# Zero pieces between the experts' weights, scatters issued as results come, and thirteen zero pieces ahead of the experts

## The chip, the cores and the metric

One core of a Trainium2 chip runs the whole kernel. The metric is the device time of one execution in microseconds (us); for the kernel before the median of three runs is shown. TensorE is called PE, VectorE DVE, ScalarE ACT, GpSimd POOL and SyncE SP, as the profile does; SP does nothing here but issue transfers, and POOL issues those with indices.

## The reference

Attention over 8 batches, 8 heads, 576 positions of 64 values, with a window of 128 and a bias by distance, and behind it a layer of experts on the 4608 tokens of 512 values: each token goes to the expert of its highest logit, an expert keeps the 80 tokens of highest gate weight, and every row of the output that no expert keeps is zero.

```python
attn_out = _attn_ref(q, k, v)
x = attn_out.transpose(0, 2, 1, 3).reshape(B * S, H * D)
logits = x @ w_gate
expert_idx = np.argmax(logits, axis=1)
out = np.zeros((N, D))
for e in range(E):
    tok_idx = np.where(expert_idx == e)[0]
    if len(tok_idx) > capacity:
        ...                        # the 80 of highest gate weight
    h = np.maximum(x[tok_idx] @ w1[e], 0.0)
    out[tok_idx] = gate_w[tok_idx, None] * (h @ w2[e])
```

## The kernel before, in words

The kernel has three stages. The attention runs as 72 units, nine to a batch; while the units of one batch run, the inputs of the next are loaded, the tokens of the one before are stored to a scratch tensor `x_dram`, and the choice of the 80 tokens of each expert is merged batch by batch. Behind the last unit comes the passage, in which the choice for the last batch is finished; a chain of small steps on DVE, ACT and PE, with idle matmuls between them. Then the eight experts run one after the other on PE: first layer (128 matmuls, line 1332), second layer (line 1358), three partial sums copied by ACT (line 1360) and the fourth added by DVE (line 1367), which makes the result `ys` of 80 rows of 512 values.

Around the experts the transfers are these. The tokens of each expert are gathered from `x_dram` by POOL (`gather`, line 1267). The weights of an expert are 4 MB (`expert_pieces`, line 656): four pieces of 512 KB for w1 and four for w2, issued by SP in this order; there is room for four experts, and the weights of expert e + 4 are issued behind the second layer of expert e (`load_expert`, lines 1361 to 1363). A result goes to the output by an indexed transfer of POOL (`scatter`, line 1312). The output must be zero elsewhere, so 36 pieces of 128 rows (256 KB each, source the tile `zero`) are written over it before any scatter may write; the scatters write to the same tensor in no known place, so each is ordered behind all writes to the output issued before it.

The list `fill` (lines 1074 to 1079) holds what SP issues when there is room: 32 half pieces of the weights of experts 0 and 1, the zero piece for the first rows of `x_dram`, and the 36 zero pieces of the output, 69 in all. `transfers(c)` (line 1132) gives up to three transfers to unit c of the attention, each with a lead, an instruction of the unit that it may not pass (`pace`, line 238); a place without a load or store takes the next of `fill`, as long as more than `LATE` are left (line 1167). The lists of `transfers` have 36 such places, so that 33 pieces are left at the end of the attention and lines 1219, 1220, 1227 and 1228 issue none. The 33 are issued all at once behind the weights of expert 7 (lines 1364 and 1365). Seven scatters are issued behind the first layer of the last expert (lines 1339 to 1341), the eighth at the end (line 1371).

Attention and passage are not issued as written. They are recorded, and a planner (`order`, line 255) puts them in order with a model of each engine's clock: at each step it takes, on the engine that can start first, the recorded operation with the lowest place in the code among those that are ready by then:

```python
t0 = max(clock[e], min(r for r, _ in rs))
...
o = min((o.key, o.at, i) for i, (r, o) in enumerate(rs) if r <= t0 + self.slack)
```

A transfer is ready when its lead, if it has one, and the operations that wrote its source are done in the model. The tile `zero` is cleared by `selection_constants` (line 637), called for unit 3. The experts are issued as written.

Of the kernel before, what the change touches and what calls it, by code (L numbers as in the profile page):

```python
# [24 lines left out]
FREE = ()  # L25

FAST = (7,)
LATE = 33


class Plan:
# [362 lines left out]
def tile_attention_then_moe(  # L394
# [15 lines left out]
    B, NP, _, S = q.shape  # L410
    H = 2 * NP
    E, DM, DF = w1.shape
# [103 lines left out]
    def load_v(b, i):  # L516
        w = H * VW
        rows = LOW if 2 * i + 1 == NKB else ALL
        return nc.sync.dma_start(
            out=vts[b % 2][rows, i].rearrange("p h c -> p (h c)"), in_=v[b][rows, w * i:w * i + w])  # L520

    def load_vt(b, g):
        if g == 0:
            vtt[b] = io.tile([P, NP, S], F32, tag="vtt", name=f"l_vt{b}", bufs=1)
        return nc.sync.dma_start(out=vtt[b][:, g], in_=vt[b, g])

    def load_k(b, g, a=0, c=S):
        return nc.sync.dma_start(out=kps[(b * NP + g) % NQ][:, a:c], in_=k[b, g, :, a:c])

    def load_q(b, g, a=0, c=S):  # L530
        if a == 0:
            qs[b, g] = io.tile([P, S], F32, tag="q", name=f"q{b}_{g}", bufs=NQ)
        return nc.sync.dma_start(out=qs[b, g][:, a:c], in_=q[b, g, :, a:c])
# [112 lines left out]
    def put_kept(b, i, k=0):  # L646
        kp = spare(i, k).bitcast(BF16)
        twice(kp[:, 0:R], at, 0, identb[0:R, 0:R])
        yield
        (nc.scalar.copy if b == LAST else nc.vector.tensor_copy)(ttt[b % 2][:, S:S + R], kp[0:2 * KS, 0:R])  # L650
# [5 lines left out]
    def expert_pieces(e, n=1):  # L656
        pool = wpools[e % 4 // 2]
        a = pool.tile([P, NC, DF], F32, tag="w1", name=f"w1_{e}")
        c = pool.tile([P, PW, DM], F32, tag="w2", name=f"w2_{e}")
        w_sb[e] = (a, c)  # L660
        s1 = w1[e].rearrange("(c p) f -> p c f", p=P)
        s2 = w2[e].rearrange("(c p) f -> p c f", p=P)

        def one(dst, src):
            return lambda: nc.sync.dma_start(out=dst, in_=src)

        w = DF // n
        m = 2 // n
        return ([one(a[:, j, w * h:w * h + w], s1[:, j, w * h:w * h + w]) for j in range(NC) for h in range(n)]
                + [one(c[:, m * j:m * j + m], s2[:, m * j:m * j + m]) for j in range(PW // m)])  # L670

    def load_expert(e):
        for piece in expert_pieces(e):
            piece()
# [182 lines left out]
    def store_x(b, u):  # L857
        return [
            nc.sync.dma_start(
                out=x_dram[P + S * b + 64 * t:P + S * b + 64 * t + 64],  # L860
                in_=xsb[b % 2][64 * j:64 * j + 64, u].rearrange("p h c -> p (h c)"))
            for j, t in enumerate(SLOT[u])]
# [211 lines left out]
    fill = []  # L1074
# [5 lines left out]
    nexp = 2  # L1080
# [6 lines left out]
    def whole(g):  # L1087
        for _ in g:
            pass
# [42 lines left out]
    def transfers(c):  # L1132
        b, r = divmod(c, CB)
        n = b + 1
        vt_ = [lambda g=g: load_vt(n if r < 8 else n + 1, g) for g in range(NP)]
        v_ = [lambda i=i: load_v(n, i) for i in range(NPR)]
        k_ = [lambda g=g: load_k(n, g) for g in range(NP)]
        q_ = [lambda g=g: load_q(n, g) for g in range(NP)]
        x_ = [lambda u=u: store_x(b - 1, u) for u in range(NU)] if b else [None] * NU
        at_ = {  # L1140
            0: [vt_[1], vt_[2]],
            1: [vt_[3], v_[0], None],
            2: [v_[1], k_[0], x_[0]],
            3: [q_[0], k_[1], x_[1]],
            4: [q_[1], v_[2], x_[2]],
            5: [v_[3], v_[4], x_[3]],
            6: [k_[2], q_[2], x_[4]],
            7: [k_[3], q_[3]],
            8: [vt_[0], None],
        }[r]  # L1150
        if b == 0 and r < 8:
            at_ = {
                2: vt_[0:1], 3: vt_[1:4], 4: [k_[0], q_[0], v_[0]], 5: [v_[1], k_[1], q_[1]],
                6: v_[2:5], 7: [k_[2], q_[2], k_[3]],
            }.get(r, [])
        elif b == 0:
            at_ = [q_[3], vt_[0], None]
        if b == LAST:
            at_ = [q for q in at_ if q in x_] + [None] * 3
            if r == 7:  # L1160
                at_ = [lambda: store_x(b, 0)] + at_
        elif b == LAST - 1 and r == 8:
            at_ = [None] * 3
        out_ = []
        for q in at_[0:3]:
            if q is None:
                q = fill.pop(0) if len(fill) > LATE and c > 4 else None
            if q:
                out_.append(q)
        return out_  # L1170
# [13 lines left out]
    for c in range(1, NCY):  # L1184
# [5 lines left out]
        if c == 3:  # L1190
            make_first_bias(2)
            make_first_bias(3)
            selection_constants()
        moves = transfers(c)
        if moves:
            nc.pace(moves.pop(0)(), marks["t", c, 1])
# [21 lines left out]
    whole(put_kept(LAST, 0))  # L1218
    for _ in range(min(4, len(fill) - LATE)):
        fill.pop(0)()  # L1220
# [4 lines left out]
    for u in range(1, NU):  # L1225
        store_x(LAST, u)
    while len(fill) > LATE:
        fill.pop(0)()
# [24 lines left out]
    def ps(tag, bufs, name):  # L1253
        return psum.tile([P, 512], F32, tag=tag, bufs=bufs, name=name)
# [44 lines left out]
    for e in range(2):  # L1299
        first = gather(e)  # L1300
    while nexp < 4:
        for piece in expert_pieces(nexp):
            tc.add_manual_dep(
                piece().ins, first.ins.name,
                mybir.DependencyInfo(mybir.DependencyClass.Sync, mybir.DependencyReason.DATA),
                reason="the first tokens before more weights")
        nexp += 1
# [4 lines left out]
    def scatter(e, ys):  # L1312
        nc.gpsimd.indirect_dma_start(  # L1313
            out=out, out_offset=bass.IndirectOffsetOnAxis(ap=sid[:, e:e + 1], axis=0),
            in_=ys, in_offset=None,
            bounds_check=NTOK - 1, oob_is_err=False,
        )

    ready = []
    for e in range(E):  # L1320
        a, c = w_sb.pop(e)
        xgT = xgTs.pop(e)
        nxt = turn(e + 1, 1) if e + 1 < E else None
        hT = work.tile([P, PW, R], F32, tag="hT", name=f"hT{e}", bufs=2)
        for f2 in range(PW // 4):
            hp = ps("s", NS, f"h{e}_{f2}")
            for fi in range(4):
                fc = 4 * f2 + fi
                for cc in range(NC):
                    for hh in range(2):  # L1330
                        f0 = P * fc + 64 * hh
                        nc.tensor.matmul(  # L1332
                            hp[64 * hh:64 * hh + 64, R * fi:R * fi + R],
                            lhsT=a[:, cc, f0:f0 + 64], rhs=xgT[:, cc],
                            start=(cc == 0), stop=(cc == NC - 1),
                        )
            nc.scalar.activation(  # L1337
                hT[:, 4 * f2:4 * f2 + 4].rearrange("p c r -> p (c r)"), hp[:, 0:4 * R], AF.Relu)
        if e == E - 1:
            for done in ready:  # L1340
                scatter(*done)
        groups = [(m0, min(R, m0 + 32)) for m0 in range(0, R, 32)]
        spread = len(groups) == 3
        own = PW * 3 // 4 if spread else PW
        yp = ps("pt", NPT, f"y{e}")
        ex = [ps(t, n, f"yx{e}_{t}") for t, n in (("d", ND), ("o", NO), ("s", NS))] if spread else []
        ys = work.tile([R, DM], F32, tag="ys", name=f"ys{e}", bufs=E)
        if nxt:
            nxt()
        for r in range(own):  # L1350
            mms = [(yp[m0:m1, 0:DM], PW - own + r, m0, m1, r == 0, r == own - 1) for m0, m1 in groups]
            if spread:
                j = r // 2
                m0, m1 = groups[j]
                mms.insert(3 * (1 - r % 2), (
                    ex[j][96:96 + m1 - m0, 0:DM], r % 2, m0, m1, r % 2 == 0, r % 2 == 1))
            for o, f_, l0, l1, st, sp in mms:
                nc.tensor.matmul(o, lhsT=hT[:, f_, l0:l1], rhs=c[:, f_], start=st, stop=sp)  # L1358
            if spread and r % 2:
                nc.scalar.copy(ys[m0:m1], ex[j][96:96 + m1 - m0, 0:DM])  # L1360
        if nexp < E:
            load_expert(nexp)
            nexp += 1
        while fill and nexp == E:
            fill.pop(0)()
        if spread:
            nc.vector.tensor_tensor(ys, ys, yp[0:R, 0:DM], ALU.add)  # L1367
        else:
            nc.vector.tensor_copy(ys, yp[0:R, 0:DM])
        ready.append((e, ys))  # L1370
# [45 lines left out]
```

## Time and profile before

| | us |
|---|---|
| median of 3 runs | 338.61 |
| lowest, highest | 338.28, 341.62 |
| profiled execution | 337.49 |
| its span, first to last instruction | 335.7 |

The profile is of one execution. Its page shares the span in 40 slices of 8.4 us and gives for each the busy share of the engines in tenths and the rate of the transfers. A busy share is an average over stages of different kinds, so a stretch is read by itself. An indexed transfer shows in POOL's timeline while it is issued; its data lands later, and the view of the transfers gives the median time from the start of the issue to the landing.

### The profile page before, as it was taken

Reading aid. Unit: us, or ns where it says so; the run is one execution under the profiler, and the core shown is the slowest. Engines: PE = TensorE matmul, PEld = TensorE weight load, DVE = VectorE, ACT = ScalarE, POOL = GpSimd, SP = SyncE. Lnnn points to the kernel's source line nnn. Section 1 sums busy time; section 2 is a strip of 40 time slices with the busy share of each in tenths; the row PEclk is TensorE's granted clock in tenths of the full one; section 3 lists DMA queues with packets and bytes.
Section 4 is the critical chain, followed back from the end, with each engine's and each line's share of the span. In section 5 each row is a group of like instructions: output and inputs, shape, how many; then the busy total and the mean of one; then the engine's idle time right before and its main releaser. Section 6 shows DMA issues by size and latency. Waiting matters only on the chain. (4 is left out here: it accounts for less than half of the span.)

```text
span 335.7 us, 15531 instructions
## 1 busy us (share of the span) xinstructions
PE 291.6 (87%) x6333; PEld 212.9 (63%) x6333; DVE 171.4 (51%) x970; ACT 160.8 (48%) x489; POOL 134.9 (40%) x358
## 2 busy tenths in 40 slices
PE   8899999999999999999999999999999999940000
PEld 6577767788778778787787788646665557610000
DVE  5566777888888789788787974101111101000000
ACT  8485766767665766667667731132222322220000
POOL 8644654855846746657558503600000000001322
PEclk9999999999999999999999999999999999995555
DMA  7969999899998998989989993799999999995121
GB/s 216 350 206 313 353 297 312 260 305 305 270 316 283 301 301 275 289 272 324 296 283 345 293 331 87 240 299 398 395 394 396 400 398 391 364 369 195 39 59 39
DMA packets 46278, 97.01 MB, mean 289 GB/s; under 512 B 5504, under 2 KB 6144, under 8 KB 46208
## 3 DMA queue, kind: packets, MB, share of 16 engines
q1 hardware_dynamic: 45184, 93.22, 81.6%
q0 software_dynamic: 1024, 2.81, 3.2%
q8 instruction: 50, 0.82, 1.0%
q14 instruction: 20, 0.16, 0.2%
HBM read 74.19 MB, written 21.81 MB: 286 GB/s over the span
## 5 line engine op out<-in xcount | busy, mean ns | idle before, releaser
L360 POOL TENSOR_SCALAR e<-e,mn 128x192 f32<-128x192 f32 (+2 forms) x216 | 87.1, 417 | 66.7 <-DVE mn L360 55.4
L360 ACT ACTIVATE ptb<-pt 128x384 f32<-128x384 f32 x144 | 64.7, 475 | 51.0 <-PE pt L360 50.1
L360 PE MATMUL av<-v,ptb 128*64 128x73 f32 (+1 forms) x2048 | 81.5, 235 | 0.9 <-issue 0.8
L360 DVE CUSTOM_DVE_ANT_0 e<-s,bneg 128x192 f32<-128x192 f32 x192 | 61.4, 354 | 35.1 <-PE s L360 26.6
L360 PEld LDWEIGHTS av<-v,ptb 128*64 128x64 f32 (+1 forms) x2048 | 64.4, 135 | 12.1 <-issue 1.3
L360 PE MATMUL s<-kp,q 64*64 64x192 f32 (+2 forms) x1152 | 60.4, 313 | 1.5 <-DMA q<-in_q_dram 1.5
L1313 POOL DMA_INDIRECT out_dram<-ys,sid x8 | 7.4, 920 | 107.7 <-DMA out_dram<-zero 90.4
L360 ACT COPY xs<-av 128x146 f32<-128x146 f32 (+1 forms) x176 | 42.9, 284 | 4.4 <-PE av L360 3.3
L1367 DVE TENSOR_TENSOR ys<-ys,y 80x512 f32<-80x512 f32 x8 | 5.5, 683 | 76.5 <-ACT ys L1360 76.5
L1358 PE MATMUL y<-w,hT 128*32 128x512 f32 (+1 forms) x288 | 43.4, 594 | 0.5 <-issue 0.5
L360 PEld LDWEIGHTS s<-kp,q 64*64 64x64 f32 x1152 | 39.1, 132 | 3.4 <-issue 1.6
L360 PE MATMUL pt<-ident,e 64*128 64x64 f32 (+1 forms) x832 | 41.0, 229 | 0.1
L1332 PEld LDWEIGHTS h<-xgTs,w 128*64 128x64 f32 x1024 | 35.9, 137 | 6.5 <-issue 6.0
L360 PEld LDWEIGHTS pt<-ident,e 64*128 64x128 f32 (+1 forms) x832 | 31.5, 135 | 11.8 <-POOL kk L360 3.1
L1332 PE MATMUL h<-xgTs,w 128*64 128x80 f32 x1024 | 37.2, 233 | 0.4 <-ACT xgTs L1296 0.4
L360 ACT ACTIVATE e<-e,mn 128x192 f32<-128x192 f32 (+1 forms) x72 | 31.2, 433 | 6.1 <-DVE mn L360 3.7
L1358 PEld LDWEIGHTS y<-w,hT 128*32 128x32 f32 (+1 forms) x288 | 10.8, 105 | 25.8 <-issue 24.8
L360 DVE DVE_READ_ACCUMULATOR2_ANT mn<- 128x1 f32 x288 | 23.9, 83 | 0.1
L360 DVE TENSOR_SCALAR_CACHE_REDUCE ncm<-s 128x272 bf16<-128x272 f32 (+7 forms) x68 | 22.7, 382 | 1.1 <-PE s L360 1.0
L1337 ACT ACTIVATE hT<-h 128x320 f32<-128x320 f32 x16 | 7.0, 437 | 29.1 <-PE h L1332 29.1
L360 DVE CUSTOM_DVE_ANT_0 e<-s,bnx 128x192 f32<-128x192 f32 (+2 forms) x64 | 17.5, 304 | 3.9 <-ACT ptb L360 3.0
L1358 PE MATMUL yx_d<-w,hT 128*32 128x512 f32 x32 | 15.2, 598 | 0.0
(144 smaller groups left out, 310.8 us busy)
## 6 DMA issues: line engine op xcount, KB each, us to landing
w<-in_moe_w_dram SPq DMA_DIRECT2D x48, 512.0 KB, 10.8
x_dram<-xs SPq DMA_DIRECT2D x72, 146.0 KB, 4.2
v<-in_v_dram SPq DMA_DIRECT2D x32, 292.0 KB, 5.0
l_vt<-in_vt_dram SPq DMA_DIRECT2D x32, 288.0 KB, 4.1
out_dram<-zero SPq DMA_DIRECT2D x36, 256.0 KB, 4.2
kp<-in_k_dram SPq DMA_DIRECT2D x31, 288.0 KB, 4.6
q<-in_q_dram SPq DMA_DIRECT2D x31, 288.0 KB, 4.9
w<-in_moe_w_dram SPq DMA_DIRECT2D x32, 256.0 KB, 4.5
```

Source lines behind the costliest of these rows:

```text
L360: c.ins = c.f(*c.args, **c.kw)
L1313: nc.gpsimd.indirect_dma_start(out=out, out_offset=bass.IndirectOffsetOnAxis(ap=sid[:, e:e + 1], axis=0), in_=ys, in_offset=None, bounds_c ...
L1332: nc.tensor.matmul(hp[64 * hh:64 * hh + 64, R * fi:R * fi + R], lhsT=a[:, cc, f0:f0 + 64], rhs=xgT[:, cc], start=(cc == 0), stop=(cc == NC ...
L1337: nc.scalar.activation(hT[:, 4 * f2:4 * f2 + 4].rearrange("p c r -> p (c r)"), hp[:, 0:4 * R], AF.Relu)
L1358: nc.tensor.matmul(o, lhsT=hT[:, f_, l0:l1], rhs=c[:, f_], start=st, stop=sp)
L1367: nc.vector.tensor_tensor(ys, ys, yp[0:R, 0:DM], ALU.add)
```

## The change

Of the 33 zero pieces that are left at the end of the attention, the lines behind the last attention unit now issue 13: four ahead of `keep_clock` and nine behind the stores of the last tokens. Twenty are left. Eight are issued behind the weights of expert 3; like those weights, they wait for the second gather. Six follow the weights of expert 4, six those of expert 5, so that the list is empty behind expert 1's second layer. A result is scattered behind the first layer of a later expert, as soon as the list is empty: results 0 and 1 in expert 2, result e - 1 in expert e. The attention takes the same 36 pieces of `fill` as before. Which zero piece goes where is not told by the rows that it clears.

```diff
-LATE = 33
+LATE, GAPS = 20, 13
...
-                q = fill.pop(0) if len(fill) > LATE and c > 4 else None
+                q = fill.pop(0) if len(fill) > LATE + GAPS and c > 4 else None
...
-        for piece in expert_pieces(nexp):
+        for piece in expert_pieces(nexp) + [fill.pop(0) for _ in range(8 * (nexp == 3))]:
             tc.add_manual_dep(
                 piece().ins, first.ins.name,
...
-        if e == E - 1:
-            for done in ready:
-                scatter(*done)
+        while ready and not fill:
+            scatter(*ready.pop(0))
...
         if nexp < E:
             load_expert(nexp)
             nexp += 1
-        while fill and nexp == E:
+        for _ in range(min(6, len(fill))):
             fill.pop(0)()
```

The lines behind the last attention unit are not changed; they follow from the smaller `LATE`:

```python
    for _ in range(min(4, len(fill) - LATE)):
        fill.pop(0)()
    keep_clock(nc.last, 150)
    ...
    for u in range(1, NU):
        store_x(LAST, u)
    while len(fill) > LATE:
        fill.pop(0)()
```

## Rows read from the trace of the kernel before

**Rows 1.** The page: span, PE in 40 slices, and the DMA's rate in them.
```profile
span 335.7 us, 15531 instructions
...
PE   8899999999999999999999999999999999940000
...
GB/s 216 350 206 313 353 297 312 260 305 305 270 316 283 301 301 275 289 272 324 296 283 345 293 331 87 240 299 398 395 394 396 400 398 391 364 369 195 39 59 39
```

**Rows 2.** Timeline of the tail: start, duration (us), engine, line [idle before it <- releaser].
```profile
298.05 0.68 DVE L1367 TENSOR_TENSOR ys<-ys,y 80x512 f32<-80x512 f32 x1 [9.18 <-ACT ys L1360]
...
307.92 0.95 POOL L1313 DMA_INDIRECT out_dram<-ys,sid  x1 [90.43 <-DMA out_dram<-zero]
...
331.61 0.91 POOL L1313 DMA_INDIRECT out_dram<-ys,sid  x1 [2.47 <-issue]
```

**Rows 3.** The scatter's line: durations in ns (least, median, most), and landing in us.
```profile
L1313 POOLq EVENT_SEMAPHORE  x12: 17/2776/2813, 304.5 to 328.1; - x12
...
DMA to landing us min/median/max: 2.6/2.6/2.6
```

**Rows 4.** Timeline of SP: the weights' first row, and the zero pieces.
```profile
212.29 27.28 SPq L665 DMA_DIRECT2D w<-in_moe_w_dram  x22
...
275.05 29.07 SPq L1079 DMA_DIRECT2D out_dram<-zero  x33
```

**Rows 5.** Windows: stretch, each engine's busy time (instructions), PE's clock, DMA share, GB/s.
```profile
core 0: us, PE busy (x) PEld busy (x) DVE busy (x) ACT busy (x) POOL busy (x), PEclk, DMA share, GB/s
...
220.00:225.00 5.00, 4.56 (x44) 1.57 (x46) 0.00 (x0) 1.16 (x2) 0.00 (x0) 1.00 1.03 283
225.00:270.00 45.00, 45.00 (x817) 28.05 (x812) 6.73 (x10) 13.18 (x26) 0.00 (x0) 1.00 1.04 396
```

**Rows 6.** Timeline of PE: the first layers of experts 6 and 7.
```profile
277.18 4.65 PE L1332 MATMUL h<-xgTs,w 128*64 128x80 f32 x128
...
287.47 4.65 PE L1332 MATMUL h<-xgTs,w 128*64 128x80 f32 x128
```

**Rows 7.** SP's issue of four weight pieces, and times to landing, in the same order.
```profile
252.80 0.37 SPq L665 DMA_DIRECT2D w<-in_moe_w_dram  x1
...
257.93 0.33 SPq L665 DMA_DIRECT2D w<-in_moe_w_dram  x1
...
w<-in_moe_w_dram SPq DMA_DIRECT2D x1, 512.0 KB, 10.5
...
268.41 0.33 SPq L665 DMA_DIRECT2D w<-in_moe_w_dram  x1
...
w<-in_moe_w_dram SPq DMA_DIRECT2D x1, 512.0 KB, 11.3
...
273.77 0.37 SPq L665 DMA_DIRECT2D w<-in_moe_w_dram  x1
...
w<-in_moe_w_dram SPq DMA_DIRECT2D x1, 512.0 KB, 11.5
```

**Rows 8.** Landing of the gathers issued at 210.2, 212.7 and 216.5 us.
```profile
xg<-x_dram,gid POOLq DMA_INDIRECT x1, 3.1
...
xg<-x_dram,gid POOLq DMA_INDIRECT x1, 8.6
...
xg<-x_dram,gid POOLq DMA_INDIRECT x1, 9.1
```

**Rows 9.** Early: the zero tile's memset, SP's next issue, and two windows as above.
```profile
14.56 0.58 POOL L360 MEMSET zero<- 128x584 f32 x1
...
17.27 4.36 SPq L360 DMA_DIRECT2D l_vt<-in_vt_dram  x4
...
15.00:20.00 5.00, 5.00 (x113) 3.68 (x113) 3.89 (x23) 2.59 (x10) 2.62 (x7) 1.00 0.70 207
20.00:25.00 5.00, 5.00 (x135) 3.83 (x128) 2.40 (x16) 4.57 (x16) 2.48 (x6) 1.00 0.68 227
```

**Rows 10.** Window behind PE's last work, columns as above.
```profile
301.20:302.00 0.80, 0.00 (x0) 0.00 (x0) 0.00 (x0) 0.00 (x0) 0.00 (x0) 0.54 1.02 384
```

## Prediction

> **What bounds the kernel now.** I read the page first: its span and its forty slices [rows 1]. PE is at 9 tenths until about 297 us and stands still for the last 38 us, while the DMA moves 364 to 400 GB/s from 227 us until about 302 us and in the last three slices 39 to 59 GB/s. The end is therefore no matter of compute. The timeline of the tail says what it is [rows 2]: the last expert's result is added on DVE at 298.05 and is ready at 298.7, but the first of the eight scatters starts at 307.92, released by the DMA of the zero pieces, and the eighth at 331.61. Seven steps take 23.7 us, 3.38 us each. The group of the scatter's line [rows 3] shows why they don't overlap: a scatter lands 2.6 us after its start, and its sequencer sits 2.78 us on a semaphore between two of them, so each scatter waits until the one before has landed, and about 0.75 us go by from the landing to the next start (3.38 less 2.6). From the last start to the end of the span are 4.1 us.
>
> SP's timeline [rows 4] gives the order of the transfers: weights from 212.29, 33 zero pieces from 275.05. The windows [rows 5] give the rate of that stream: 396 GB/s from 225 to 270 with PE busy in all of it. So a zero piece (262144 bytes) is 0.66 us of DMA, 33 of them 21.8 us, and both streams, PE's and the DMA's, are full at once. The tail of 37 us (298.7 to 335.7) is 9.2 us of waiting for zeros, 23.7 us of chained scatters, and 4.1 us of end.
>
> **The zeros that leave the tail.** Thirteen pieces move ahead of the experts, twenty go between weights: eight behind expert 3, six behind expert 4, six behind expert 5. All twenty are ahead of expert 6 in SP's one queue. Expert 5's last piece was issued at 252.80 and landed 10.5 us later, at 263.3 [rows 7]; with twenty zeros ahead of or just behind it the last zero lands at 263.3 + 20 x 0.66 = 276.5 instead of about 307. The first scatter can start at 276.5 + 0.75 = 277.3; results 0 to 5 are there by then or a microsecond later.
>
> **What the twenty cost the experts.** Expert 6's first layer needs its four w1 pieces, the last issued at 257.93 and landed 10.5 us later, 268.4; now 268.4 + 13.2 = 281.6. Its first matmul was at 277.18 [rows 6], so PE waits 4.4 us where it had 8.8 us in hand. Expert 7's w1 was complete at 268.41 + 11.3 = 279.7 [rows 7], now at 292.9 and with one scatter's 164 KB (0.4 us) 293.3; it would start at 287.47 + 4.4 = 291.9, so 1.4 us more. Expert 5 is on the edge: its w1 comes one expert (4.19 MB at 396 GB/s, 10.6 us) ahead of expert 6's in the old order, at 257.8, now 14 zeros or 9.3 us later at 267.1, and it starts 10.29 us ahead of expert 6, at 266.9. Expert 4, another 10.6 and 10.29 us earlier, has eight zeros, 5.3 us, against 9.4 in hand: nothing. In all PE ends 5.8 us later, and the last result is ready at 298.7 + 5.8 = 304.5.
>
> In that wait PE does a pair of matmuls per landed piece and no more. In the tail of before the granted clock had fallen from the upper to the lower level by 301.2 to 302 (mean 0.54), about 4 us behind PE's last work [rows 10]. If it falls in the wait of expert 6 too, its first layer (4.65 us) takes up to twice as long: the result at 309.2. As will be seen, that still lies ahead of the scatter that waits for it.
>
> **What the earlier scatters cost.** They are issued from POOL, which has nothing else to do here, so a blocked scatter blocks nobody. But now they run while SP keeps eight weight pieces of 512 KB in flight, and they stay chained, since all write the same tensor. The trace has no scatter under load. Its nearest rows are the gathers, the same kind of transfer on the same queue [rows 8]: 3.1 us alone, 8.6 us for the first one issued after the weights had begun, 9.1 us for the last. From below the bound is the 2.6 us of a lone scatter, from above the 9.1 us. I take the gather's 8.6 less the half microsecond by which a lone scatter is quicker: 8.1, a step of 8.85 us.
>
> The weights end at 273.77 + 11.5 = 285.3 [rows 7], now 285.3 + 13.2 + 0.8 (two scatters' data) = 299.3. Then: scatter 0 at 277.3, 1 at 286.1, 2 at 295.0. The third has only 4 us of load left, between 2.6 and 8.1: I take 5.0, so scatter 3 at 300.8. From there on 3.38 each: 304.1, 307.5, 310.9, and scatter 7 at 314.3. Its result was ready at 304.5 (309.2 with a fallen clock), so the chain decides and the wait of PE is hidden under it. End: 314.3 + 4.1 = 318.4, against 335.7: 17.3 us less.
>
> A rule bears on this. The Trainium skill, "DMA: Bandwidth & Descriptors", section "Queues, rings and completion order", says that each DMA engine takes turns between the queues that have work, one packet at a time. By it a scatter wouldn't stand behind what SP has outstanding, its step would stay near that of a lone one, and the end would be the one of the first rival below. The trace speaks against it so far: the gather's 8.6 us beside 3.1.
>
> **The thirteen.** They are named "in the passage", in the code behind the last attention unit. But the planner orders each queue by what is ready, and these pieces have no lead and read only the zero tile, so they are ready as soon as its memset is done, at 15.1 us [rows 9]. A piece with a lower place in the code wins when both are ready; the zeros fill each idle moment of SP. I expect them from about 15 us on, among the loads of the second batch, where SP idles between loads and the DMA engines are busy only 0.70 and 0.68 of the time [rows 9]. From 15 to 25 us about 3.1 us of DMA are free, five zeros; the other eight, 5.3 us, are spread over later gaps or push loads back. Price: from nothing to 5.3 us if all of the rest reached PE; loads are issued two or three units ahead, so I take 0.5 us. Wherever they go, they leave the tail; their 8.6 us are in the 13.2 against 21.8 above.
>
> **Sum.** 335.7 - 17.3 + 0.5 = 318.9 us of span, 16.8 less. The profiled execution took 337.49 (1.8 beyond its span), so 320.7 for it; the median of the runs shown is 338.61, 1.1 more. On the median: 338.61 - 16.8 = 321.8, predicted 322.
>
> **Rivals.** (1) Scatters stay short under load, by the rule of turns. With 2.6 us the chain would be at its eighth at 277.3 + 7 x 3.38 = 301.0, before the last result; the end is then PE's: 304.5 + 0.4 + 4.1 = 309.0, with 0.5 for the loads 26.2 less, 312.4. With a step of 5 us, midway: scatters at 277.3, 282.3, 287.3, 292.3, 297.3 and from 301.5 on by 3.38, eighth at 308.3, end 312.4, total 315.8. For it: a scatter moves only 164 KB, 0.4 us at the stream's rate; against it: [rows 8].
> (2) The thirteen do stand in the passage, or the loads pushed back reach PE. In the passage the DMA has a hole (one slice of 87 GB/s) [rows 1], but four pieces go ahead of the last token stores, 2.6 us, and the gathers behind nine more would land later than 3.1 us, by up to the 5.5 us between a lone and a loaded one [rows 8]. The experts start 1.5 to 6 us later: 323 to 328.
> (3) Slower than before: zeros written and scattered between weights break the stream. From 220 to 225, with gathers among the weights, it ran at 283 GB/s instead of 396 [rows 5]. The stream from 212.3 is 32 MB (48 weight pieces, 20 zeros, six gathers, some scatters), 23 MB of it up to the last zero. At 283 GB/s that zero lands at 293.5, the weights end at 325, three scatters take 8.85 us each, the fourth 5.75, and the eighth starts at about 337: end 341, a total of 344. At 300 GB/s the eighth starts at 331.6, as before: that is the point from which it decides. Against it: the dip lasted 5 us.
>
> **Chances.** The forecast, chain under load, 319.5 to 326: 0.60. Short scatters, 311 to 319.5: 0.24. Passage or late loads, 323 to 332: 0.11, half of it within the first's span. Broken stream: 0.05. The range holds the first two and what of the third lies near: 312 to 327. A change of about 1% is what a measurement of this kernel can tell from none; faster by over 1% (under 335.2) is all but the last case and a sliver: 0.94, the same 0.03, slower 0.03.
>
> **What would show it.** Scatter 0 starts near 277 and the next ones about 9 us apart while weights flow, then 3.4; PE waits for weights before experts 6 and 7 and not before; the last scatter starts over 5 us behind the last add; thirteen zero pieces stand in SP's timeline between 15 and 60 us. I am wrong if scatters under load land in under 5 us, if the last add is what releases the last scatter, or if PE waits for loads in the attention for more than 3 us.

## The result, and the profile after

The changed kernel takes 324.39 us (median of four runs, 323.02 to 325.47) beside 338.62 us for the kernel before: a ratio of 0.956 (95% interval 0.949 to 0.962). The profiled execution took 324.34 us with a span of 322.6. Predicted were 322, with 318.9 for the span. A ratio is taken over fewer executions than the median beside it (unusually slow ones are left out), so it is not exactly the quotient of two medians.

The page of the changed kernel, in the lines of [rows 1] and with PE's clock:

```profile
span 322.6 us, 15529 instructions
...
PE   9999999999899999999999999998999999959930
...
PEclk9999999999989999999999999999999999988985
...
GB/s 223 362 304 345 340 317 297 330 321 316 318 255 279 342 316 285 267 268 299 322 284 289 329 272 317 285 59 277 320 400 393 364 396 401 402 403 402 243 45 41
```

PE now works until about 309 us, 13 us before the end (38 us in the kernel before), and the stretch at 39 to 59 GB/s behind the zeros has become two slices at 41 to 45. PE's clock dips in slice 12 and in slices 36 and 37, where it was even before. The hole of the passage is still there, at 59 GB/s.

The timeline of the changed kernel, with the lines that answer to [rows 2]: the first gather, the scatters on POOL, and the last add on DVE.

```profile
212.82 1.19 POOL L1270 DMA_INDIRECT xg<-x_dram,gid  x1 [3.80 <-DVE sid L1261]
...
283.41 0.95 POOL L1313 DMA_INDIRECT out_dram<-ys,sid  x1 [60.42 <-DMA w<-in_moe_w_dram]
290.02 0.93 POOL L1313 DMA_INDIRECT out_dram<-ys,sid  x1 [5.66 <-issue]
297.29 0.91 POOL L1313 DMA_INDIRECT out_dram<-ys,sid  x1 [6.33 <-issue]
304.47 0.91 POOL L1313 DMA_INDIRECT out_dram<-ys,sid  x1 [6.27 <-issue]
308.30 0.91 POOL L1313 DMA_INDIRECT out_dram<-ys,sid  x1 [2.92 <-issue]
...
309.79 0.68 DVE L1366 TENSOR_TENSOR ys<-ys,y 80x512 f32<-80x512 f32 x1 [9.18 <-ACT ys L1359]
...
318.46 0.91 POOL L1313 DMA_INDIRECT out_dram<-ys,sid  x1 [2.48 <-issue]
```

The chain of scatters starts at 283.4 instead of 307.9, its first three steps are 6.6, 7.3 and 7.2 us long instead of 3.4, and its last scatter still starts eight microseconds behind the last result (310.5). So the chain sets the end, as before. The first row tells of something else: the first gather starts at 212.8, 5.4 us later than in the kernel before, though nothing of the attention's own work has changed. The same row of the kernel before:

```profile
207.41 1.19 POOL L1270 DMA_INDIRECT xg<-x_dram,gid  x1 [3.79 <-DVE sid L1261]
```

### The profile page after: what moved, and what is told of

Read it like the earlier page. It is cut to its first block, busy times and chain, and to the rows that moved or that the text cites. A ratio compares the mean times of both kernels' runs of the same rounds, so it can differ in the third digit from the quotient of the medians.

```text
span 322.6 us, 15529 instructions
## 1 busy us (share of the span) xinstructions
PE 297.9 (92%) x6333; PEld 217.0 (67%) x6333; DVE 171.2 (53%) x970; ACT 160.8 (50%) x489; POOL 134.4 (42%) x358
## 5 line engine op out<-in xcount | busy, mean ns | idle before, releaser
L360 PE MATMUL s<-kp,q 64*64 64x192 f32 (+2 forms) x1152 | 61.9, 316 | 1.0 <-DMA q<-in_q_dram 0.5
L1332 PEld LDWEIGHTS h<-xgTs,w 128*64 128x64 f32 x1024 | 37.8, 141 | 10.8 <-issue 6.6
L1332 PE MATMUL h<-xgTs,w 128*64 128x80 f32 x1024 | 39.7, 239 | 4.0 <-DMA w<-in_moe_w_dram 3.0
L360 PE MATMUL pt<-ident,e 64*128 64x64 f32 (+1 forms) x832 | 42.0, 230 | 0.6 <-issue 0.4
L360 PEld LDWEIGHTS s<-kp,q 64*64 64x64 f32 x1152 | 39.8, 133 | 3.8 <-issue 1.4
```

What stands on the lines that cost most here:

```text
L360: c.ins = c.f(*c.args, **c.kw)
L1332: nc.tensor.matmul(hp[64 * hh:64 * hh + 64, R * fi:R * fi + R], lhsT=a[:, cc, f0:f0 + 64], rhs=xgT[:, cc], start=(cc == 0), stop=(cc == NC ...
```

## Experiments

Times are medians of four or six runs; each ratio is to the kernel before on the same chip. Single executions of the kernels below lie up to 1.4% to either side of their median. A profile is of one execution, so a difference of two or three microseconds in one profile is read only together with the others.

**The thirteen left out.**

```diff
-    for _ in range(min(4, len(fill) - LATE)):
-        fill.pop(0)()
...
-    while len(fill) > LATE:
-        fill.pop(0)()
+    del fill[:GAPS]
```

> The thirteen zero pieces that the changed kernel issues among the loads of the attention are left out altogether (1664 rows of the output are not cleared by the kernel); all else is as changed. Theory A: these transfers are what makes the attention 5.4 us longer in the changed kernel (gathers from 212.8 instead of 207.4). Then the gathers start at 207.4 again, the stream of weights and 20 zeros and the chain of scatters move 5.4 us forward unchanged, and the time is 324.4 - 5.4 = 319. Theory B: the 5.4 us are scatter between executions, or come from elsewhere. Then the gathers start near 212 and the time stays near 324.

319.13 us, ratio 0.946 (0.940 to 0.953). The first gather in its profile, on POOL:

```profile
206.92 1.19 POOL L1267 DMA_INDIRECT xg<-x_dram,gid  x1 [3.79 <-DVE sid L1258]
```

The attention ends as in the kernel before. By the ratios, 0.946 beside 0.956, the kernel is some 3 us quicker than the changed one; theory A is favoured, though the intervals overlap a little.

**The same places, small pieces.**

```diff
-        fill.pop(0)()
+        i = NTOK // P - len(fill)
+        fill.pop(0)
+        nc.sync.dma_start(out=out[P * i:P * i + 16], in_=zero[0:16, 0:DM]).op.cost = 4.0 * P * DM / 360.0
```

> The thirteen early zero pieces keep their places in SP's queue and every engine keeps its order, but each clears 16 rows (32 KB) instead of 128 (1456 rows of the output are not cleared). Theory A1: the bytes of the thirteen, 3.4 MB among the attention's loads, cost the attention its 3 to 5 us. Then the gathers start as in the kernel that leaves them out, at 206.5 to 207.5, and the time is 319. Theory A2: the changed order (the planner moves a few loads and matmuls for them, each takes a place among eight transfers in flight) costs it. Then the gathers start at 210 to 213 as in the three profiles with the thirteen, and the time is 321 to 324.

319.21 us, ratio 0.941 (0.934 to 0.948); the first gather:

```profile
208.76 1.20 POOL L1275 DMA_INDIRECT xg<-x_dram,gid  x1 [3.79 <-DVE sid L1266]
```

Every engine's order is that of the changed kernel, but with an eighth of the bytes the time is that of the kernel that leaves them out, and this interval lies below that of the changed kernel (it just touches that of its repeat below). By the time it is the bytes, not the places in the queue (A1). The first gather, at 208.8, doesn't decide: it lies between the 207.5 of A1 and the 210 of A2.

**The thirteen in the passage.**

```diff
     while len(fill) > LATE:
-        fill.pop(0)()
+        nc.pace(fill.pop(0)(), gate_exp[LAST])
```

(and nothing ahead of `keep_clock`)

> The thirteen pieces are given a lead in the passage (the exponential of the last batch's gate), so that they are issued behind the stores of the last tokens, from about 202.5 us on. Attention and planner's order are then those of the kernel before. Theory A: the attention ends as in the kernel before (gathers start at 207.4), the thirteen take 8.6 us of the DMA between 202.5 and 212, the gathers land 1 to 2 us later than alone, the rest follows as in the changed kernel: 324.4 - 5.4 + 0 to 2 = 319 to 321. Theory B: no gain from the place, 324, and more if the gathers stand behind the zeros (8.6 us instead of 3.1: up to 330).

320.72 us, ratio 0.951 (0.943 to 0.959). The first gather:

```profile
206.55 1.19 POOL L1268 DMA_INDIRECT xg<-x_dram,gid  x1 [3.79 <-DMA out_dram<-zero]
```

It starts where it did in the kernel before. This kernel is 1.6 us behind the one without the thirteen, timed beside it. That may be the price of the passage, but the intervals overlap widely. The changed kernel and this one were timed once more side by side, six runs each:

> The changed kernel once more, on the same chip as the three below, for the comparison: about 324, a ratio of 0.956 to the kernel before. If PE's unexplained waits in the attention are late instruction blocks (each of them so far ended 1.35 to 1.6 us behind the end of a 16 KB packet of the instruction queue), every such wait over half a microsecond in this profile ends that far behind one too.

> The thirteen in the passage, once more, beside the changed kernel on one chip: if the thirteen cost the attention 3 to 4 us and the passage 1 to 2, it is 2 to 3 us faster than the changed kernel, a ratio of 0.948 to 0.951; if the first difference was chance, they are equal.

323.09 us (0.9536, 0.9479 to 0.9593) for the changed kernel and 321.15 us (0.9463, 0.9416 to 0.9510) with the thirteen in the passage. The medians differ by 2 us, the ratios by 0.007, some 2.5 us, and the intervals overlap, so the gain is likely and not certain; in this profile of the changed kernel the first gather started at 208.7. So the price of the thirteen changes from one execution to the next. Over all profiles, the first gather of the five kernels or repeats with all thirteen early starts at 212.8, 210.9, 210.1, 211.7 and 208.7 (mean 210.9), that of the eight without their bytes there at 207.4, 206.9, 206.6, 208.8, 209.0, 210.3, 208.6 and 205.5 (mean 207.9): some 3 us, though the two groups overlap.

**The scatters' place in the code undone.**

```diff
-        while ready and not fill:
+        while ready and e == E - 1:
             scatter(*ready.pop(0))
```

> Only the place of the scatters in the code is undone: seven of them again behind the first layer of the last expert; the zero pieces stay as changed. Theory C: POOL has nothing else to do, so the place in the code sets no time; a scatter starts when the zeros, its result and the scatter before it have landed. Then scatter 0 starts at about 283 as in the changed kernel and the time is the same, 324. Theory D: the place counts, scatters wait for the last expert (first layer ends at 293.6). Then the chain starts 10 us later, two of its loaded steps become lone ones, and the time is 327 to 331.

323.03 us (318.59 to 324.17), and the chain on POOL as in the changed kernel:

```profile
281.24 0.95 POOL L1313 DMA_INDIRECT out_dram<-ys,sid  x1 [60.18 <-DMA w<-in_moe_w_dram]
288.05 0.93 POOL L1313 DMA_INDIRECT out_dram<-ys,sid  x1 [5.86 <-issue]
295.46 0.91 POOL L1313 DMA_INDIRECT out_dram<-ys,sid  x1 [6.48 <-issue]
```

PE's first row of expert 6 in this kernel:

```profile
284.38 0.89 PE L1332 MATMUL h<-xgTs,w 128*64 128x80 f32 x12
```

Scatter 0 starts at 281.2, before expert 6 has begun, though its line stands behind expert 7's first layer. Theory C holds: POOL runs ahead to its first wait. The executions lie too far apart for a ratio, but none reaches the 327 us of theory D. "Scatters as results come" changes nothing that shows here; the gain comes from where the zeros are.

**Half the bytes in flight ahead of a scatter.**

```diff
-        for piece in expert_pieces(e):
+        for piece in expert_pieces(e, 2 if e > 5 else 1):
```

> The weights of experts 6 and 7 are loaded in pieces of 256 KB instead of 512 KB; SP keeps eight pieces in flight, so half the bytes are ahead of a scatter. Theory E: a scatter under load stands behind what is in flight (steps of 6.6 to 7.2 us in the changed kernel). Then its step falls to about 5 us: scatters at 283.4, 288.5, 293.6, 298.7, 303.8 and every 3.4 us from there, eighth at 314, the time about 4 us less, 320. Theory F: scatters and weights take turns at the DMA engines whatever is in flight; the step stays at 6.6 to 7.2 us and the time at 324.

321.42 us, ratio 0.954 (0.947 to 0.960). First the time to landing of the weight pieces that are issued from 283.9 to 293 us, beside the scatters, in the changed kernel:

```profile
w<-in_moe_w_dram SPq DMA_DIRECT2D x7, 512.0 KB, 11.6
```

then in this one, same stretch, with its scatters:

```profile
w<-in_moe_w_dram SPq DMA_DIRECT2D x13, 256.0 KB, 5.7
```

```profile
281.61 0.95 POOL L1313 DMA_INDIRECT out_dram<-ys,sid  x1 [61.30 <-DMA w<-in_moe_w_dram]
287.89 0.93 POOL L1313 DMA_INDIRECT out_dram<-ys,sid  x1 [5.33 <-issue]
294.82 0.91 POOL L1313 DMA_INDIRECT out_dram<-ys,sid  x1 [6.00 <-issue]
302.05 0.91 POOL L1313 DMA_INDIRECT out_dram<-ys,sid  x1 [6.32 <-issue]
305.42 0.91 POOL L1313 DMA_INDIRECT out_dram<-ys,sid  x1 [2.46 <-issue]
```

A piece waits half as long, so half as much is in flight; the scatter's steps are 6.3, 6.9 and 7.2 us, as before. Theory E, mine, falls: a scatter doesn't stand behind what SP has in flight. The chain from first to last start is 33.9 us here and 35.3 in the kernel with late scatters, timed beside it; the medians differ by 1.6 us.

**No weights behind the last zero.**

```diff
-        a, c = w_sb.pop(e)
+        a, c = w_sb[e if e < 6 else e - 2]
...
-        if nexp < E:
+        if nexp < 6:
             load_expert(nexp)
```

> The changed kernel, but the weights of experts 6 and 7 aren't loaded; experts 6 and 7 compute with those of 4 and 5 (their rows of the output are other values). Nothing is left in the stream behind the last zero. Theory I: the stream of weights is what makes a scatter's step 6.6 to 7.2 us. Then all steps are 3.4 us from the first on: scatter 0 at 280 to 283, scatter 7 23.7 us later, at 304 to 307, or half a microsecond behind the last add if that is later; PE doesn't wait for experts 6 and 7 and adds at 303: time 310 to 313. The rival, that a step is long for something else in the first three scatters (results read while PE writes): steps as in the changed kernel, scatter 7 at 316 to 318, 322 to 324.

312.58 us, ratio 0.922 (0.915 to 0.929). The scatters, and the last add:

```profile
283.61 0.95 POOL L1313 DMA_INDIRECT out_dram<-ys,sid  x1 [61.89 <-DMA out_dram<-zero]
287.05 0.93 POOL L1313 DMA_INDIRECT out_dram<-ys,sid  x1 [2.49 <-issue]
...
304.52 0.68 DVE L1366 TENSOR_TENSOR ys<-ys,y 80x512 f32<-80x512 f32 x1 [9.18 <-ACT ys L1359]
...
307.36 0.92 POOL L1313 DMA_INDIRECT out_dram<-ys,sid  x1 [2.46 <-issue]
```

All seven steps are 3.4 us, from the same start. The stream of weights is what makes a step twice as long (theory I).

**The twenty earlier in the stream.** With the thirteen in the passage, fourteen behind expert 3 and six behind expert 4, and then all twenty behind expert 3; shown is the edit for all twenty, the other has 14 in its place:

```diff
-        for piece in expert_pieces(nexp) + [fill.pop(0) for _ in range(8 * (nexp == 3))]:
+        for piece in expert_pieces(nexp) + [fill.pop(0) for _ in range(20 * (nexp == 3))]:
```

> The thirteen stand in the passage, as in e2, and the twenty go 14 behind the weights of expert 3 and 6 behind those of expert 4, so the last zero lands one expert's weights (10.6 us) earlier. Theory H: the last zero's landing starts the chain of scatters, which sets the end, and a scatter under load takes 7 us. Then scatter 0 at 267.9 instead of 278.5, five loaded steps, scatter 7 at 309 instead of 314, and the time 320.7 - 4.8 = 316. The rival, that the last result or the end of the weights sets the end: no change, 320 to 321.

> As e6_14_6, but all twenty behind the weights of expert 3. Theory H: scatter 0 at about 257, the chain then has time to wait for its results, and the last scatter starts half a microsecond behind the last add, at about 306: 320.7 - 8 = 313. PE's wait for weights moves to expert 4 (4 us late) and is the same in sum. The rival: seven scatters under load slow the weights by more than their bytes, PE waits again before experts 6 and 7, and the last add moves from 305.6 to 308 or later: 315 to 318.

> Thirteen in the passage and twenty behind expert 3, once more: the last scatter is released by the last add, so the chain no longer sets the end and PE does; 314 to 316, a ratio of 0.925 to 0.935, 8 us less than the changed kernel.

14 and 6: 317.61 us, ratio 0.939 (0.931 to 0.948). Scatter 0 starts at 271.1, the first five steps are 5.6 to 7.6 us long and the eighth scatter starts at 311.1, 2 us behind the last result: the chain still sets the end, and an earlier start brings it forward, though by less than the start. All twenty: 315.94 us (312.77 to 319.35), ratio 0.925 (0.917 to 0.934), and once more 315.25 us, 0.931 (0.927 to 0.935). The end of the repeat, on DVE and POOL, and what PE waited for behind 225 us:

```profile
305.85 0.68 DVE L1364 TENSOR_TENSOR ys<-ys,y 80x512 f32<-80x512 f32 x1 [9.72 <-ACT ys L1357]
...
306.81 0.91 POOL L1311 DMA_INDIRECT out_dram<-ys,sid  x1 [5.64 <-DVE ys L1364]
```

```profile
PE h L1330 <- DMA w<-in_moe_w_dram: 4.2, 6, 1.0
```

The last scatter is released by the last add: the chain no longer sets the end (theory H). What is left is PE, which waits for weights. Here the rival has a share: from the first gather to the last add are 300.3 us, 2 to 3 more than in the two profiles with the thirteen in the passage (298.4 and 297.5), PE waits before experts 6 and 7 too, and the medians lie in the rival's 315 to 318 and not at 313.

**Seven early, thirteen in the passage, thirteen behind expert 3.**

```diff
-    for _ in range(min(4, len(fill) - LATE)):
+    for _ in range(7):
         fill.pop(0)()
...
-    while len(fill) > LATE:
-        fill.pop(0)()
+    while len(fill) > 13:
+        nc.pace(fill.pop(0)(), gate_exp[LAST])
...
-        for piece in expert_pieces(nexp) + [fill.pop(0) for _ in range(8 * (nexp == 3))]:
+        for piece in expert_pieces(nexp) + [fill.pop(0) for _ in range(13 * (nexp == 3))]:
```

> Seven pieces early among the attention's loads, thirteen in the passage, thirteen behind expert 3. If PE sets the end and its wait for weights is what the zeros ahead of them exceed 8.8 us by, thirteen (8.6 us) leave no wait before expert 4 and little behind it: 4 to 6 us less than e7_again, for about 2 us more in the attention (7 pieces at the 0.26 us that a piece of the thirteen cost): 311 to 313. If the seven cost the attention what the thirteen did, or the scatters' data makes PE wait anyway, 314 to 317.

313.09 us (311.09 to 315.31), ratio 0.922 (0.917 to 0.926): the fastest whole kernel here, 10 us below the changed one beside it. Its end and its wait for weights:

```profile
308.37 0.68 DVE L1366 TENSOR_TENSOR ys<-ys,y 80x512 f32<-80x512 f32 x1 [10.25 <-ACT ys L1359]
...
309.33 0.92 POOL L1313 DMA_INDIRECT out_dram<-ys,sid  x1 [5.56 <-DVE ys L1366]
```

```profile
PE h L1332 <- DMA w<-in_moe_w_dram: 1.8, 3, 0.8
```

The median is at the upper edge of the first bet's 311 to 313, but the gain over the twenty behind expert 3 is 2 us (3 by the ratios, whose intervals don't overlap), not the 4 to 6 of that bet: in this profile, which is of the longest of its six executions, the attention is late again (first gather at 211.3), and some wait for weights is left.

## Why the prediction was right, and where its sum was off

The step that decided, that the chain of scatters behind the last zero sets the end before and after, is shown. Its last start was forecast at 314.8 with the half microsecond for the loads and came at 318.5. Three terms make the difference: 4.9 more for the attention, 0.7 for a later last zero, 2.0 less for the steps. Two errors of opposite sign, so the sum was, by luck, better than its parts.

**The last zero and the first scatter: right.** Forecast at 277.3; measured 283.4, of which 5.4 are the attention's. Without these it is 278.0, against 277.3.

**The cost to the experts: sum right, one term in another's place.** The forecast had expert 6 wait 4.4 us, expert 7 1.4 more and the last result come 5.8 us later, and expert 5 on the edge. PE's first layers of experts 5 (its last 116 matmuls), 6 and 7 in the changed kernel, and a window behind expert 6's wait, columns as in [rows 5]:

```profile
273.36 4.23 PE L1332 MATMUL h<-xgTs,w 128*64 128x80 f32 x116 [0.33 <-DMA w<-in_moe_w_dram]
...
283.92 0.36 PE L1332 MATMUL h<-xgTs,w 128*64 128x80 f32 x4 [0.61 <-ACT ys L1359]
285.11 0.36 PE L1332 MATMUL h<-xgTs,w 128*64 128x80 f32 x4 [0.83 <-DMA w<-in_moe_w_dram]
286.39 0.36 PE L1332 MATMUL h<-xgTs,w 128*64 128x80 f32 x4 [0.93 <-DMA w<-in_moe_w_dram]
287.69 5.87 PE L1332 MATMUL h<-xgTs,w 128*64 128x80 f32 x116 [0.94 <-DMA w<-in_moe_w_dram]
...
299.21 4.65 PE L1332 MATMUL h<-xgTs,w 128*64 128x80 f32 x128
```

```profile
288.60:291.90 3.30, 3.30 (x55) 3.30 (x52) 0.00 (x0) 0.44 (x1) 0.93 (x1) 0.50 1.06 397
```

Expert 5 waited 0.3 us. For expert 6 PE did four matmuls for each piece that lands (the forecast said a pair), 1.3 us apart, and full work from 287.7, 5.1 us behind 277.2 + 5.4. Behind the wait the clock was at its lower level (0.50) in the window shown, and 116 matmuls took 5.87 us, where the same number took 4.23 for expert 5; the forecast named that and left it out of the 304.5. Expert 7 then waited for no weights: its 1.4 us didn't come, and the 1.6 us of the slower clock stand in their place. The last result was ready at 310.5; the forecast 304.5 plus the attention's 5.4 is 309.9. That the two terms are alike is luck. The result lay under the chain, as forecast, and costs nothing.

**A scatter under load: direction right, size and reason wrong.** I took 8.85 us for a step from the gathers [rows 8]; it was 6.6 to 7.3, and the third step was full length (7.2, forecast 5.75). That makes 35.05 us from the first to the last start instead of 37.0. The reason, that a scatter stands behind the eight pieces in flight, fell with the half pieces. I had said that the trace speaks against taking turns between queues. The half pieces don't: a scatter doesn't stand behind what is outstanding, just as by turns it wouldn't. But the short step that I had drawn from the turns didn't come either. The runs only show that a scatter is slow while the stream runs, with all or half of it in flight, and quick without it. Why it takes 6.4 us to land instead of 2.6 is left open.

**The thirteen: place right, price wrong.** They stand in SP's timeline of the changed kernel where the planner's rule puts them, from 14 us on and not in the passage:

```profile
14.28 0.42 SPq L360 DMA_DIRECT2D out_dram<-zero  x1
...
16.52 1.44 SPq L360 DMA_DIRECT2D out_dram<-zero  x3
...
106.10 0.90 SPq L360 DMA_DIRECT2D out_dram<-zero  x2
...
108.64 0.67 SPq L360 DMA_DIRECT2D out_dram<-zero  x1
```

I had expected them done by about 60 us; they reach to 109. The failed step is "I take 0.5", where 5.4 us were measured in this profile and some 3 in the mean: I looked for loads that come late, and from 10 us to the end of the attention no matmul of PE waited for a load. Its longest waits have no releaser in the profile ("issue"). The longest of them and the next (PE's rows, then for each the instruction queue in the DMA's view of a stretch just before it):

```profile
85.43 0.25 PE L360 MATMUL s<-at,oa 80*80 80x6 bf16 x3 [1.47 <-issue]
...
113.36 0.29 PE L360 MATMUL av<-v,ptb 64*64 64x73 f32 x3 [0.88 <-issue]
```

```profile
q8 instruction: 1, 0.02, 38.8%
...
q8 instruction: 1, 0.02, 36.7%
```

The second fence is of the stretches 82.95 to 83.1 and 110.95 to 111.1 us: one 16 KB packet of the queue that carries instructions begins in each. 38.8% of sixteen DMA engines over 0.15 us is 0.93 us, so the first, begun at 83.02, ended at 83.95, and PE stood from 83.96 to 85.43. In all fourteen profiles, PE has twenty waits of more than half a microsecond between 10 and 200 us without a releaser, and every one ends 1.35 to 1.60 us behind the end of such a packet. My reading is that PE stands because its next instructions aren't there. In the five profiles with all thirteen early, these waits sum to 3.2, 3.3, 1.9, 4.3 and 0.7 us (mean 2.7); in the eight without, to 1.2, 1.5 and 0.8 in three and nothing in five (mean 0.4); with seven early, to 2.1. That is 2.2 of the 3 us between the two groups. That the waits are for instructions is inferred from these coincidences and not shown; it wasn't tried to move the instruction blocks themselves. For the thirteen's bytes as what brings them on speak the difference between the groups, the experiment with small pieces, and the times: of the thirteen waits in the five profiles, seven begin 3.8 to 5.4 us behind the issue of one of the thirteen pieces. The other six begin 10 to 61 us behind, and what brings those on stays open. In this profile the first wait cost more than itself. Two windows of the changed kernel:

```profile
84.00:86.00 2.00, 0.57 (x14) 0.53 (x15) 0.53 (x4) 0.00 (x0) 1.14 (x3) 1.00 1.01 353
87.20:90.50 3.30, 3.30 (x53) 2.37 (x46) 1.99 (x15) 1.60 (x6) 2.03 (x8) 0.50 0.78 203
```

PE worked 0.57 of two microseconds, and from 87.1 to 90.5 its clock was at the lower level: the dip in the page's slices. Around them the attention lost 3 us against the kernel before, by the starts of its units' exponentials on ACT.

**The rivals.** The short scatter didn't come; with no weights behind the zeros it is there at once. Of the second rival, the passage didn't come; a price in the attention of more than half a microsecond did, not by late loads but, by the reading above, for the most part by late instructions, and the measured 324.4 lies in its span of 323 to 328. The stream didn't break: it ran at 364 to 403 GB/s with zeros and scatters in it.

## What to carry to other kernels

Transfers whose data nobody reads still set the end when everything that writes to the same tensor is chained behind the last of them: put them where the last one lands early, then check which chain is the next to end last. The place of a line in the code need not be the time of its work: the planner put the thirteen pieces where it found them ready, and a scatter on an idle queue starts when what it waits for is done. And a transfer in a gap isn't free when the DMA engines are already busy for 0.92 of their time (the kernel before, 10 to 200 us): price it by what shares the engines, which by the reading above includes the instructions.

## What the runs showed of the hardware

A scatter of 164 KB lands in 2.6 us alone and in 5.8 to 6.5 us beside a stream of weights at 400 GB/s; with half as much of the stream in flight the steps of the chain are as long (6.3 to 7.2 us). Instructions come through the DMA engines too, in packets of 16 KB on their own queue, one every 5 us in the attention; twenty waits of PE, of 0.5 to 1.5 us, end just behind one, and are read here as waits for instructions. The Trainium skill, "Runtime: NRT & Kernel Launch", section "Instruction fetch mechanics", says that a long kernel streams its instructions in 16 KB blocks by DMA and that the cost is mostly hidden. The trace agrees on the blocks, and in the kernel before on the hiding (no such wait of over half a microsecond); in the profile of the changed kernel, by this reading, 3.2 us weren't hidden.
